# One attention place per visit, with the outputs in G1's PSUM banks, in a fused retention and MLP kernel

## The chip, the core and the metric

The kernel runs on one core of a Trainium2 chip. The metric is the device time of one execution in microseconds; lower is better. TensorE (PE in the profile) multiplies matrices into PSUM, VectorE (DVE) and ScalarE (ACT) read PSUM and write SBUF, GpSimd (POOL) works on SBUF and issues the loads, and SyncE (SP) issues the stores.

## The reference

```python
# q, k, v: 8 batches x 8 heads x 576 positions x 64
scores = scale * np.matmul(q, k.transpose(0, 1, 3, 2))
Dmat = np.where(rel >= 0, gamma[:, None, None] ** rel[None, :, :], 0.0)   # rel = i - j
ret = scores * Dmat[None, :, :, :]
attn_out = np.matmul(ret, v)
x = attn_out.transpose(0, 2, 1, 3).reshape(8 * 576, 512)     # 4608 tokens
h = x @ w_in                                                 # 512 -> 2048
g = h * np.tanh(log1p(exp(h)))                               # Mish
out = g @ w_out                                              # 2048 -> 512
```

The decay of a head is a power of the distance, so earlier positions enter a block through a running state (the sum of k times v), and only pairs within a block need scores.

## The kernel before

**Chunks and tiles.** Each batch is cut into blocks of 128 positions; the last 64 positions of two batches share a block. That gives 36 chunks of 128 tokens. The first 8 are the first blocks of the 8 batches and need no state. Then, for each pair of batches, come three blocks of each and the shared one. Four chunks make a tile of 512 tokens, so there are 9 tiles.

**Steps of a chunk n** (`att(n, steps)`):
- P (L273): VectorE scales q into one half of the tile qks; k is loaded straight into the other half.
- V (L279): GpSimd scales v into vs.
- T: transposes q and k into qkT. For chunks below NPE = 18, TensorE does it (L288, eight 128x128 matmuls) and ScalarE copies the result (L289). From 18 on it is a DMA transpose in SyncE's queue (L291).
- S (L301): 16 small matmuls with 64 rows of weights give the scores in two PSUM banks (pool ps_sc, tile sc). VectorE multiplies them by the mask into sm (L305).
- O: 16 matmuls add state times q (L353; twice as many in the first half for the shared block) and vs times sm (L358). The result is a part of xT, the MLP's input.

`state(upto)` runs at most one step of the states, and nothing where chunk `upto` already has its state: eight matmuls with 64 columns of weights (L333) add into the bank st, which VectorE then reads out to ssb (L336). The first step of a batch reads the tile k0, the others a chunk's qks and vs.

**Per tile of tokens.** `g1(t, f)` multiplies 128 of the 2048 hidden columns: four 128x512 matmuls (L371) into one of two banks (pool ps_h, tile hp), and ScalarE applies Mish (L373). `g2(t, i)` is a quarter of a 128-token output: four 128x512 matmuls (L386) into the one bank ops (pool ps_o). After the fourth quarter the result waits in `ready`, and the next `stores()` has VectorE copy it (L422) and SyncE send it off.

**PSUM.** The eight banks are: two scores tiles of two banks, one st, two hp and one ops.

**Order.** All engines run in the order in which the code issues (manual schedule). After a start-up for the first two tiles, the main loop has phases t = 2 to 9, each with 16 steps i. In a step, G1 of tile t runs ahead of a quarter of G2 of tile t-1; in phase 2, G2 (of tile 1) runs in every second step only, and phase 9 has no G1. Eight steps are a visit (w = i % 8) and serve two chunks, n and n+1, of tile t+1: n = 12, 14 in phase 2, 16, 18 in phase 3, and so on up to 34 in phase 7. Phase 8 has no attention. Before the change a visit has two attention places: the scores of n and n+1 at w = 0 and their outputs at w = 4. In both kernels a quarter that ends an output of G2 falls on w = 3 and w = 7 from phase 3 on, so `stores()` has work at w = 4 and w = 0.

**Where outputs go.** In phase 1 `step_o` (tile index 2) uses the bank ops; later ones use the first bank of the chunk's own scores tile, which the product has emptied. VectorE casts them to xT (L362).

**Buffers that matter.** qks has nine buffers, qkT five, vs five, sm three, ssb six, the stored result four.

Of the kernel before, what the change touches and what calls it, by code (L numbers as in the profile page):

```python
# [10 lines left out]
F32 = mybir.dt.float32  # L11
# [6 lines left out]
def kernel(  # L18
# [18 lines left out]
    nc = tc.nc  # L37
    B, H, S, D = q.shape
    assert (B, H, S, D) == (8, 8, 576, 64)
    P = 128  # L40
    NP = H // 2
# [5 lines left out]
    NPE = 18  # L47
# [10 lines left out]
    n_chunks = len(chunks)  # L58
# [15 lines left out]
    ps_h = ctx.enter_context(tc.tile_pool(name="ps_h", bufs=2, space=PS))  # L74
    ps_o = ctx.enter_context(tc.tile_pool(name="ps_o", bufs=1, space=PS))
# [94 lines left out]
    xts = {}  # L170
# [76 lines left out]
    def load_k0(b):  # L247
        k0[b] = first.tile([P, H, D], BF16, name="k0", bufs=B)
        nc.gpsimd.dma_start(out=k0[b], in_=k[b, :, 0:P, :].rearrange("h p d -> p h d"))
# [69 lines left out]
    def state(upto):  # L319

        if upto >= n_chunks or done[0] > state_of[upto]:
            return False
        b, c = states[done[0]]
        done[0] += 1
        if c == 0:
            ks, vs = k0[b], v0s[b]
            st_ps[b] = ps_st.tile([P, NP, 64], F32, name="st")
        else:
            ks, vs = live[index[b, c]]["qks"][:, 1], live[index[b, c]]["vs"]
        st = st_ps[b]  # L330
        for p in range(NP):
            for e in range(2):
                nc.tensor.matmul(st[ds(64 * e, 64), p, :], lhsT=ks[:, 2 * p + e, :], rhs=vs[:, 2 * p + e, :],  # L333
                                 start=(c == 0 and p == 0), stop=True, skip_group_check=True)
        ssb = tr.tile([P, 2, NP, 64], BF16, name="ssb", bufs=6)
        nc.vector.tensor_tensor(  # L336
            ssb.rearrange("p e n d -> p e (n d)"),
            st.rearrange("p n d -> p (n d)").unsqueeze(1).to_broadcast([P, 2, NP * 64]),
            diag.unsqueeze(2).to_broadcast([P, 2, NP * 64]), op=OP.mult)
        st_sb[b, c] = ssb  # L340
        return True

    def step_o(n):
        b, c = chunks[n]
        t, s = divmod(n, NCH)
        assert done[0] > state_of[n]
        qk, vs, sc, sm = (live[n][x] for x in ("qk", "vs", "sc", "sm"))
        ot = ps_o.tile([P, NP, P], F32, name="ops") if t == 2 else sc[:, 0]
        halves = [(0, P, b, c - 1)] if c < 4 else [(0, 64, b, 3), (64, 64, b + 1, 3)]
        for i0, iw, bb, cc in halves:  # L350
            for p in range(NP):
                for e in range(2):
                    nc.tensor.matmul(ot[ds(64 * e, 64), p, ds(i0, iw)], lhsT=st_sb[bb, cc][:, e, p, :],  # L353
                                     rhs=qk[:, 0, p, ds(i0, iw)],
                                     start=(i0 == 0 and p == 0), stop=False, skip_group_check=True)
        for p in range(NP):
            for e in range(2):
                nc.tensor.matmul(ot[ds(64 * e, 64), p, :], lhsT=vs[:, 2 * p + e, :], rhs=sm[:, e, p, :],  # L358
                                 start=False, stop=True, skip_group_check=True)
        if s == 0:  # L360
            xts[t] = xp.tile([P, KC, NCH * P], BF16, name="xT")
        nc.vector.tensor_copy(xts[t][:, :, ts(s, P)], ot)  # L362

    outs = {}

    def g1(t, f, cols=slice(0, NCH * P)):
        if t not in gts:
            gts[t] = gp.tile([P, nF, NCH * P], BF16, name="gT")
        hp = ps_h.tile([P, NCH * P], F32, name="hp")
        for c in range(KC):  # L370
            nc.tensor.matmul(hp[:, cols], lhsT=w_in_t[:, c, ts(f, P)], rhs=xts[t][:, c, cols],  # L371
                             start=(c == 0), stop=(c == KC - 1))
        nc.scalar.activation(gts[t][:, f, cols], hp[:, cols], AX.Mish)  # L373

    def g2(t, i):
        s, part = divmod(i, 4)
        if t == nT - 1:
            s = (s + 3) % 4
        if part == 0:
            if (t == nT - 1 and s % 2) or (t == 1 and s < 2):  # L380
                outs[t] = ps_h.tile([P, d_model], F32, name="hp")
            else:
                outs[t] = ps_o.tile([P, d_model], F32, name="ops")
        ops = outs[t]
        for f in range(4 * part, 4 * part + 4):
            nc.tensor.matmul(ops, lhsT=gts[t][:, f, ts(s, P)], rhs=w_out_t[:, f, :],  # L386
                             start=(f == 0), stop=(f == nF - 1))
        if part == 3:
            ready.append((t, s, ops))
# [3 lines left out]
    def stores():  # L393
        while ready:
            store(*ready.pop(), nc.vector.tensor_copy)
# [24 lines left out]
    def store(t, s, ops, copy):  # L420
        ot = op.tile([P, d_model], F32, name="res")
        copy(ot, ops)  # L422
        b, c = chunks[NCH * t + s]
        if c < 4:
            nc.sync.dma_start(out=out[ds(b * S + P * c, P), :], in_=ot)
        else:
            for e in range(2):
                nc.sync.dma_start(out=out[ds((b + e) * S + 512, 64), :], in_=ot[ds(64 * e, 64), :])

    def att(n, steps):  # L430
        if n >= n_chunks:
            return
        for step in steps:
            {"P": step_p, "V": step_v, "T": step_t, "S": step_s, "O": step_o}[step](n)

    dve, act, pool = nc.vector.tensor_copy, nc.scalar.copy, nc.gpsimd.tensor_copy
# [63 lines left out]
    for i in range(nF):  # L500
        for step in steps.get(i, "").split():
            n = int(step[1])
# [17 lines left out]
    def more_loads(upto):  # L520
        for _ in range(2):
            if queued[0] <= upto:
                load(queued[0])
                queued[0] += 1
# [4 lines left out]
    for u in range(24):  # L529
        j, w = divmod(u, 4)  # L530
# [32 lines left out]
    for t in range(2, nT + 1):  # L563
        for i in range(nF):
            n, w = NCH * (t + 1) + i // 8 * 2, i % 8
            if t in (3, 4) and i in (4, 12):
                load_k0(2 * t - 2 + i // 8)
            by_pe = n + 2 < NPE
            if w == 0:
                stores()  # L570
                state(n + 1)
                att(n, "S")
                att(n + 1, "S")
            if w == 4:
                state(n + 3)
                stores()
                att(n, "O")
                att(n + 1, "O")
                state(n + 3)
            if by_pe and w in (1, 3):  # L580
                att(n + 2 + w // 2, "P")
            if w in (0, 1):
                att(n + 2 + w, "V")
            if w in (4, 5):
                more_loads(n + w - 2 + PF)
            if w - (5 if by_pe else 0) in (0, 1):
                att(n + 2 + (w == 1 or w == 6), "T")
            if w == 7 and n + 4 >= NPE:
                att(n + 4, "P")
                att(n + 5, "P")  # L590
            stores()
            if t < nT:
                g1(t, i)
            if t == 2:
                if i % 2:
                    g2(1, 8 + i // 2)
            elif t < nT or i < 12:
                g2(t - 1, i)
# [32 lines left out]
```

## Time and profile before

| | us |
|---|---|
| median of three runs | 312.92 (312.32 to 312.98) |
| the profiled execution: its own time | 313.61 |
| its span in the trace | 311.9 |
| TensorE busy | 300.3 |
| VectorE, ScalarE, GpSimd busy | 137.1, 110.7, 143.6 |
| G1 matmuls (L371) busy | 141.3, x562 |
| G2 matmuls (L386) busy, into ops and hp | 110.1 and 14.7 |
| the 24 casts of L362 from sc | 15.3, 0.68 each |

How to read it: a line of a timeline begins with the start in microseconds from the span's start and a busy time, then the engine, the source line, the operation, what it writes and reads, and how many instructions are merged; in square brackets stands the idle time ahead and what ended it. Matmuls overlap and their ends are modelled, so lengths on TensorE are read from start to start. A few matmul records are missing (x3 where four were issued).

### The profile page before, as it was taken

What the parts mean: (1) busy time and instruction counts of PE and PEld (TensorE: products, weight loads), DVE (VectorE), ACT (ScalarE), POOL (GpSimd) and SP (SyncE); (2) the same over time, 40 slices, a digit from 0 to 9 for tenths busy, and PEclk for the clock granted to TensorE, in tenths of its full rate; (3) what the DMA queues carried; (4) which work ended last, traced back from release to release, by engine and by line L of the source; (5) the groups of instructions that cost most, each with busy time, mean ns of one, the idle gap of its engine ahead of it and who ended that gap; (6) DMA issues with size and microseconds to landing.
All of it is one profiled execution on the core that took longest, in us unless ns stands there. A gap on an engine that the chain in (4) does not pass through costs nothing.

```text
span 311.9 us, 5809 instructions
## 1 busy us (share of the span) xinstructions
PE 300.3 (96%) x2429; PEld 152.3 (49%) x2468; DVE 137.1 (44%) x200; ACT 110.7 (36%) x183; POOL 143.6 (46%) x178
## 2 busy tenths in 40 slices
PE   7769999999999999999999999999999999999995
PEld 3444554555465554545454444545454544444444
DVE  4723455778637635443434453535354332001111
ACT  4546345671453623233333333232323333333300
POOL 8578849989985976274726262612010000000000
PEclk9999999999999999999999999999999999999999
DMA  7999999999995999999996949371504100010031
GB/s 177 234 206 205 220 208 221 256 171 175 232 203 96 148 181 191 155 195 146 179 178 116 189 88 218 77 144 37 101 36 101 36 34 36 35 34 34 36 101 68
DMA packets 73642, 42.85 MB, mean 137 GB/s; under 512 B 58640, under 2 KB 64528, under 8 KB 73616
## 3 DMA queue, kind: packets, MB, share of 16 engines
q0 software_dynamic: 48640, 27.27, 61.1%
q1 hardware_dynamic: 24832, 15.08, 23.3%
q8 instruction: 19, 0.31, 0.5%
q10 hardware_dynamic: 144, 0.13, 0.1%
q14 instruction: 7, 0.06, 0.1%
HBM read 38.80 MB, written 9.44 MB: 155 GB/s over the span
## 4 chain that ended last, share of the span: by engine, by line
PE 92%; issue 2%; DMA 2%; POOL 2%; DVE 0%; ACT 0%; POOLq 0%; ACTq 0%
PE hp L371 39%; PE ops L386 30%; PE hp L386 4%; PE sc L301 3%; PE st L333 3%; DMA gT<-in_v_dram 2%; PE hp L403 2%; PE sc L353 2%; PE sc L358 2%; PE sc L288 1%; PE st L403 1%; PE ops L403 1%; PE hp L414 1%; POOL gT L106 1%; POOL vb L222 1%
## 5 line engine op out<-in xcount | busy, mean ns | idle before, releaser
L371 PE MATMUL hp<-xT,w_in_t 128*128 128x512 bf16 (+1 forms) x562 | 141.3, 373 | 2.2 <-DVE xT L239 0.8
L373 ACT ACTIVATE gT<-hp 128x512 bf16<-128x512 f32 (+1 forms) x148 | 86.8, 586 | 156.4 <-PE hp L371 144.2
L386 PE MATMUL ops<-w_out_t,gT 128*128 128x512 bf16 x430 | 110.1, 379 | 0.4
L371 PEld LDWEIGHTS <-w_in_t 128*128 128x128 bf16 x592 | 55.1, 98 | 61.9 <-DVE xT L239 1.3
L386 PEld LDWEIGHTS <-gT 128*128 128x128 bf16 x496 | 48.2, 98 | 58.1 <-issue 0.8
L422 DVE COPY res<-ops 128x512 f32<-128x512 f32 x28 | 19.3, 688 | 82.7 <-PE ops L386 79.7
L279 POOL TENSOR_TENSOR vs<-vraw,gv 128x512 bf16<-128x512 f32 x28 | 30.3, 1096 | 51.8 <-PE sc L358 37.6
L336 DVE TENSOR_TENSOR ssb<-st,diag 128x512 bf16<-128x512 f32 x32 | 21.9, 685 | 47.2 <-PE st L333 47.2
L305 DVE TENSOR_TENSOR sm<-sc,mask 128x1024 bf16<-128x1024 f32 x28 | 33.0, 1215 | 6.2 <-PE sc L301 6.2
L263 POOL DMA_DIRECT2D qraw<-in_q_dram x24 | 21.8, 910 | 12.8 <-DVE qks L273 9.6
L263 POOL DMA_DIRECT2D vraw<-in_v_dram x24 | 21.8, 908 | 2.9 <-DMA vpair<-in_v_dram 1.5
L263 POOL DMA_DIRECT2D qks<-in_k_dram x24 | 21.8, 906 | 1.3 <-DMA w_out_t<-in_moe_w_out_dram 0.9
L273 DVE TENSOR_TENSOR qks<-qraw,gq 128x512 bf16<-128x512 f32 x28 | 20.2, 758 | 0.0
L362 DVE CAST xT<-sc 128x512 bf16<-128x512 f32 x24 | 15.3, 680 | 0.0
L386 PE MATMUL hp<-w_out_t,gT 128*128 128x512 bf16 x61 | 14.7, 379 | 0.2
L289 ACT COPY qkT<-sc 128x1024 bf16<-128x1024 bf16 x10 | 10.1, 1010 | 8.0 <-PE sc L288 8.0
L215 DVE TENSOR_TENSOR sm<-sc,dmask 128x1024 bf16<-128x1024 f32 x8 | 9.4, 1220 | 5.0 <-PE sc L211 5.0
L353 PE MATMUL sc<-qkT,ssb 128*64 128x128 bf16 (+1 forms) x224 | 9.5, 213 | 0.0
L358 PE MATMUL sc<-sm,vs 128*64 128x128 bf16 x192 | 9.4, 219 | 0.0
L301 PE MATMUL sc<-qkT 64*128 64x128 bf16 x224 | 9.0, 218 | 0.0
L403 PEld LDWEIGHTS <-gT 128*128 128x128 bf16 x64 | 5.8, 98 | 6.5
L267 POOL DMA_DIRECT2D qraw<-in_q_dram x8 | 5.6, 706 | 7.3 <-DVE qks L273 7.3
(103 smaller groups left out, 192.0 us busy)
## 6 DMA issues: line engine op xcount, KB each, us to landing
out_dram<-res SPq DMA_DIRECT2D x31, 256.0 KB, 3.0
qraw<-in_q_dram POOLq DMA_DIRECT2D x24, 256.0 KB, 6.0
vraw<-in_v_dram POOLq DMA_DIRECT2D x24, 256.0 KB, 6.8
qks<-in_k_dram POOLq DMA_DIRECT2D x24, 128.0 KB, 6.4
w_in_t<-in_moe_w_in_dram POOLq DMA_DIRECT2D x4, 512.0 KB, 11.1
w_out_t<-in_moe_w_out_dram POOLq DMA_DIRECT2D x4, 512.0 KB, 9.8
gT<-in_q_dram SPq DMA_DIRECT2D x4, 256.0 KB, 4.9
gT<-in_k_dram POOLq DMA_DIRECT2D x8, 128.0 KB, 6.3
```

The costliest lines, as they stand in the source:

```text
L263: nc.gpsimd.dma_start(out=t, in_=src[b, :, ds(P * c, P), :].rearrange("h p d -> p h d"))
L273: nc.vector.tensor_tensor(live[n]["qks"][:, 0], live[n]["q"], gq[:, c, :].unsqueeze(2).to_broadcast([P, H, D]), op=OP.mult)
L279: nc.gpsimd.tensor_tensor(vs, live[n]["v"], gv[:, c, :].unsqueeze(2).to_broadcast([P, H, D]), op=OP.mult)
L301: nc.tensor.matmul(sc[:, e, p, :], lhsT=qk[r, 1, p, :], rhs=qk[r, 0, p, :], start=True, stop=True)
L305: nc.vector.tensor_tensor(sm.rearrange("p e n i -> p (e n) i"), sc.rearrange("p e n i -> p (e n) i"), m.unsqueeze(1).to_broadcast([P, 2 * ...
L336: nc.vector.tensor_tensor(ssb.rearrange("p e n d -> p e (n d)"), st.rearrange("p n d -> p (n d)").unsqueeze(1).to_broadcast([P, 2, NP * 64 ...
L353: nc.tensor.matmul(ot[ds(64 * e, 64), p, ds(i0, iw)], lhsT=st_sb[bb, cc][:, e, p, :], rhs=qk[:, 0, p, ds(i0, iw)], start=(i0 == 0 and p == ...
L371: nc.tensor.matmul(hp[:, cols], lhsT=w_in_t[:, c, ts(f, P)], rhs=xts[t][:, c, cols], start=(c == 0), stop=(c == KC - 1))
L373: nc.scalar.activation(gts[t][:, f, cols], hp[:, cols], AX.Mish)
L386: nc.tensor.matmul(ops, lhsT=gts[t][:, f, ts(s, P)], rhs=w_out_t[:, f, :], start=(f == 0), stop=(f == nF - 1))
L403: nc.tensor.matmul(outs[0, s], lhsT=gts[0][:, f, ts(s, P)], rhs=w_out_t[:, f, :], start=(f == 0), stop=(f == nF - 1))
L422: copy(ot, ops)
```

## The change

A visit keeps one attention place, at w = 6: a state, the outputs of n and n+1, another state, then the scores of n+2 and n+3, and a third state where one is due. The first scores (chunks 12 and 13) stay at the start of phase 2. From chunk 12 on, outputs go into two hp banks, and ScalarE casts them. Transposes on TensorE move from w = 5 and 6 to w = 2 and 4. The DMA transposes of n+4 and n+5 go to w = 7 and to w = 0 of the next visit, where those of n+2 and n+3 were at w = 0 and 1; the scaling P of n+4 and n+5 moves from w = 7 to w = 4 and 5. What is computed stays the same, and so does the number of instructions on TensorE.

```diff
@@ step_o
-        ot = ps_o.tile([P, NP, P], F32, name="ops") if t == 2 else sc[:, 0]
+        pool, name = (ps_o, "ops") if t == 2 else (ps_h, "hp")
+        ot = pool.tile([P, NP, P], F32, name=name)
...
-        nc.vector.tensor_copy(xts[t][:, :, ts(s, P)], ot)
+        (nc.vector.tensor_copy if t == 2 else nc.scalar.copy)(xts[t][:, :, ts(s, P)], ot)
@@ main loop
-            by_pe = n + 2 < NPE
-            if w == 0:
+            if t == 2 and i == 0:
                 stores()
                 state(n + 1)
                 att(n, "S")
                 att(n + 1, "S")
-            if w == 4:
-                state(n + 3)
-                stores()
+                state(n + 1)
+            if w == 6:
+                state(min(n + 4, n_chunks - 1))
                 att(n, "O")
                 att(n + 1, "O")
+                state(min(n + 4, n_chunks - 1))
+                att(n + 2, "S")
+                att(n + 3, "S")
                 state(n + 3)
-            if by_pe and w in (1, 3):
+            if w in (1, 3) and n + 2 < NPE:
                 att(n + 2 + w // 2, "P")
+            if w in (4, 5) and n + 4 >= NPE:
+                att(n + w, "P")
             if w in (0, 1):
                 att(n + 2 + w, "V")
             if w in (4, 5):
                 more_loads(n + w - 2 + PF)
-            if w - (5 if by_pe else 0) in (0, 1):
-                att(n + 2 + (w == 1 or w == 6), "T")
+            if w in (2, 4) and n + 2 < NPE:
+                att(n + 1 + w // 2, "T")
             if w == 7 and n + 4 >= NPE:
-                att(n + 4, "P")
-                att(n + 5, "P")
+                att(n + 4, "T")
+            if w == 0 and n + 2 >= NPE:
+                att(n + 3, "T")
             stores()
```

## Prediction

> **What bounds the kernel now.** I read the page first: the engines, then the chain that ended last.
>
> ```profile
> PE 300.3 (96%) x2429; PEld 152.3 (49%) x2468; DVE 137.1 (44%) x200; ACT 110.7 (36%) x183; POOL 143.6 (46%) x178
> ...
> PE 92%; issue 2%; DMA 2%; POOL 2%; DVE 0%; ACT 0%; POOLq 0%; ACTq 0%
> ```
>
> TensorE is busy 96% of the span and is 92% of the chain; no other engine reaches half. So the change is worth only what it does to TensorE's gaps, and gaps of hundredths of a microsecond, repeated per visit, are the whole matter. The granted clock is 1.00 in every stretch from 80 us on, so one price per matmul holds. I therefore read TensorE's timeline by the starts of its groups. In the steady phases groups of four 512-column matmuls (G1 on L371, G2 on L386) start 0.863 us apart. Everything above that at an attention place is the place's price. One visit of before, with the outputs first and the scores 8 us later:
>
> ```profile
> 129.39 1.03 PE L386 MATMUL ops<-w_out_t,gT 128*128 128x512 bf16 x4
> 130.35 0.32 PE L333 MATMUL st<-vs,qks 128*64 128x64 bf16 x8
> ...
> 131.17 0.39 PE L358 MATMUL sc<-sm,vs 128*64 128x128 bf16 x8
> 131.54 0.32 PE L333 MATMUL st<-vs,qks 128*64 128x64 bf16 x8
> 131.79 1.04 PE L371 MATMUL hp<-xT,w_in_t 128*128 128x512 bf16 x3
> ...
> 137.84 1.03 PE L386 MATMUL ops<-w_out_t,gT 128*128 128x512 bf16 x4
> 138.80 0.62 PE L301 MATMUL sc<-qkT 64*128 64x128 bf16 x16
> 139.36 0.82 PE L371 MATMUL hp<-xT,w_in_t 128*128 128x512 bf16 x3
> ```
>
> The reader is to see three things. The G2 group ahead of a place takes 0.96 us (129.39 to 130.35, 137.84 to 138.80) instead of 0.86: 0.10 for going from 128x128 weights to halves of the array. The scores take 0.55 (138.80 to 139.36). The second state starts 1.19 after the first.
>
> **The merge.** A scores place alone costs 137.84 to 139.36, 1.52, less the group's 0.86: 0.66. What scores cost when they follow a state is shown where a state stands ahead of them in before:
>
> ```profile
> 121.58 1.03 PE L386 MATMUL ops<-w_out_t,gT 128*128 128x512 bf16 x4
> 122.54 0.32 PE L333 MATMUL st<-vs,qks 128*64 128x64 bf16 x8
> 122.78 0.62 PE L301 MATMUL sc<-qkT 64*128 64x128 bf16 x16
> 123.34 1.04 PE L371 MATMUL hp<-xT,w_in_t 128*128 128x512 bf16 x3
> ```
>
> The state lasts 0.25 there, as it does when G1 follows it (131.54 to 131.79), and the scores 0.55 again. So behind the second state of an output place the scores add 0.55, and each merge saves 0.66 - 0.55 = 0.11 (an entry of 0.10 and 0.01 in the first G1 group behind it). Of the 12 visits (chunks 12 to 34), 11 have scores to bring along; in the order of the changed kernel 8 of them hold two states: 8 x 0.107 = 0.86 us saved. (0.107 by starts in nanoseconds.)
>
> The Trainium skill, page "TensorEngine Tiling (Array Packing)", section "Key Properties", says that a change of tiling mode drains the array, and "TensorE: Matmul & The Clock Gate", section "Single matmul latency", puts the fixed part of a warm matmul at about 166 ns. By that estimate the 8 merges would save 1.4 and the final sum would be some 0.5 lower. I take the 0.10 of the rows, which are of just these shapes.
>
> **Three visits with a third state.** Before, three scores places have a state ahead of them, as above, at 121.58 to 123.34 less 0.86 = 0.90. In the changed order that state comes last, behind the scores (chunks 16, 22 and 30). It writes the one st bank, so it must wait until VectorE has read the second state out. VectorE does that in 0.69:
>
> ```profile
> 130.70 0.69 DVE L336 TENSOR_TENSOR ssb<-st,diag 128x512 bf16<-128x512 f32 x1 [4.51 <-PE st L333]
> ```
>
> From one state's start to the next one's this wait makes 1.19 where the second reads qks (130.35 to 131.54), and 1.10 where it reads k0 (114.18 to 115.28). Behind the second state lie only 0.25 + 0.55 = 0.80 of state and scores, so TensorE stands for 0.30 to 0.39. The place grows by 1.10 or 1.19 and loses the 0.90 elsewhere: +0.29, +0.20 (chunk 22, a k0) and +0.29, together +0.78. Queued behind the waiting state are G1 and all else of TensorE. The scores' products wait on VectorE behind the second ssb, but need some 3.4 us in all and have 4.3 until the next copy of ops, so they delay nothing.
>
> **The ops bank loses its cover.** This is the largest term. G2 has one PSUM bank (ops); every fourth step VectorE must copy it before G2 may start again. In phases 3 to 7 that falls on steps with w = 0 and w = 4, and there before puts exactly its two attention places between the old group and the new one. The change empties both and moves all to w = 6. Then only one G1 group, 0.86, lies between. Phase 8 of before, which has no attention left, shows that case:
>
> ```profile
> 266.77 1.03 PE L371 MATMUL hp<-xT,w_in_t 128*128 128x512 bf16 x4
> 267.72 1.02 PE L386 MATMUL ops<-w_out_t,gT 128*128 128x512 bf16 x4
> ```
>
> ```profile
> 266.98 0.69 DVE L422 COPY res<-ops 128x512 f32<-128x512 f32 x1 [6.17 <-PE ops L386]
> ```
>
> 266.77 to 267.72 is 0.95, not 0.86: the copy starts 0.04 behind the last matmul's end, takes 0.69, and G2 starts 0.05 after it. The four turnovers there cost 0.083, 0.082, 0.081 and 0.082. Five phases with four turnovers each are newly bare: 20 x 0.082 = 1.64 us added. (Phase 2 runs two G1 groups between and keeps its cover.) Bounds: nothing, if the copy were ready sooner; 0.13, if its start lagged by 0.09 as one copy of before did (matmul end 106.68, start 106.77).
>
> **Outputs in G1's banks, copied by ScalarE.** The cast takes 0.585 on ScalarE (row of the groups by line, below) against 0.68 on VectorE.
>
> ```profile
> L239 ACT CAST xT<-hp 128x512 bf16<-128x512 f32 x1 | 0.6, 585 | 1.3 <-PE hp L236 1.3
> ```
>
> Counted from the place's start, the first output's matmuls end at 0.86; with 0.04, 0.585 and 0.05 its bank is free at 1.54. G1 wants it at 2.0 or later, behind the other output, the second state and the scores: hidden, with 0.45 to spare. The second copy ends at 2.1, and its bank is wanted 0.86 (phase 2) or 1.73 later. The Mish behind the copies then starts on time. On the other side, the second output needs the bank of the G1 group before last; its Mish ends about when the place begins, 0.7 ahead of need. Only the last place (chunks 34 and 35) has neither states nor scores as cover: in before it runs from 258.72 to 259.86, its first output ends at 259.45, and 259.45 + 0.68 = 260.12, so +0.27. If the cover were gone everywhere, 11 x 0.27 more.
>
> On VectorE 24 casts of 0.68 disappear. The page "TensorEngine Tiling (Array Packing)", section "PSUM Bottleneck", advises ScalarE and VectorE together for emptying PSUM. Here VectorE stood idle for 3.8 us or more before the copies of w = 0 and for 6.2 before the bare ones of phase 8, so its casts held nobody: booked at nothing.
>
> **Transposes, products and loads.** PE transposes (0.45 each, eight 0.056 matmuls) move from w = 5, 6 to 2, 4 in phase 2 without any mode change. DMA transposes move past one output store in SyncE's queue; the first of a pair leaves when its qks is scaled, the second once the first output of the place has read its buffer.
>
> ```profile
> DMA to landing us min/median/max: 3.1/6.0/11.8
> ```
>
> From that output to the scores of the next place are over 14 us, against 11.8 at worst: nothing. VectorE's scaling moves to w = 4, 5, ahead of a store; in its queue it follows the store of w = 0 and runs then, on loads that landed long before (chunk 18's at 88 us, for a product at about 96). GpSimd's vs waits two steps longer for the outputs but no longer for the scaling; its next loads leave about as before, and are wanted some 25 us later. Both at nothing; each microsecond that one lacks would be TensorE's.
>
> **Sum.** -0.86 + 0.78 + 1.64 + 0.27 = +1.83 us. The profiled execution takes 313.61 (span 311.9 and 1.7 around it) and would become 315.4; it lies 0.7 above the median of the three runs. On the median 312.92 the forecast is 314.8. About 0.2%, 0.6 us, can be told from no change here.
>
> **Rivals.**
> 1. Faster: VectorE's round trip shortens as its casts leave, and the bare copies and third states cost less. Each turnover shortens by x up to 0.08, each third state by x up to 0.4. It decides at x = 0.08: -0.86 + 0 + 0.54 + 0.27 = -0.05; at x = 0.4 the time is 312.92 - 0.86 - 0.3 + 0.27 = 312.0. For it: 24 casts fewer. Against: the copies already found VectorE idle. Faster 0.05, between the two 0.06.
> 2. Slower still: a transpose pair lands after its scores are due. It decides at about 14 us of landing; the first pairs took 9.5 to 11.8 while the DMA engines were 90% busy, and now start closer to the loads. One or two late pairs at 1 to 2 us: 316 to 318. Chance 0.06.
> 3. Slower still: ScalarE's copies come late in every visit. It decides beyond 0.45 us of delay; 11 visits at 0.1 to 0.3 give 1 to 3 us: 316 to 318. Against: ScalarE is idle 1.13 before every Mish. Chance 0.06.
> The forecast has 0.77. Its own bounds: turnovers at 0.05 and third states at 0.5 in all give 313.9; turnovers at 0.13 give 315.8. The range 313.7 to 315.9 leaves out the two slow rivals and most of the first. Chances: faster 0.05, same 0.06, slower 0.89.
>
> **What would show it.** G2's first matmul at w = 0 and w = 4 of phases 3 to 7 starts 0.95 after the G1 group's first, not 0.86: the main step. In 8 places the scores follow the second state at 0.25 and last 0.55. In three places the last state starts 0.3 to 0.4 behind the scores' end. G1 behind the last place is 0.27 later. A G1 group that waits on ScalarE in an ordinary place, scores that wait on a transpose, or turnovers at 0.86 would make the prediction wrong.

## The result, and the profile after

The changed kernel takes 315.64 us (median of six runs, 315.03 to 316.39), the kernel before 312.74 on the same chip (six runs, 312.23 to 313.39): ratio 1.0095, 95% interval 1.0075 to 1.0115. The forecast was 314.8, in a range of 313.7 to 315.9. The profiled execution took 315.03, with a span of 313.3 and a granted clock of 1.00. The engines and the chain, from the page after:

```profile
PE 303.4 (97%) x2468; PEld 153.2 (49%) x2468; DVE 125.8 (40%) x176; ACT 123.8 (40%) x207; POOL 143.0 (46%) x178
...
PE 90%; issue 2%; DMA 2%; DVE 2%; POOL 2%; ACT 1%; POOLq 0%; DVEq 0%; ACTq 0%
```

The 24 casts have gone from VectorE (x200 before) to ScalarE (x183 before), and TensorE is still the bound. That TensorE's busy time rose from 300.3 says little, as 2468 of its matmul records are in this trace and 2429 were in the one before. What did change is the chain: VectorE now holds 2% of it and ScalarE 1%, where both rounded to 0%.

The time ahead of phase 2 varies by up to 3 us between executions (in the ten that were profiled, its first G1 group started between 79.0 and 82.0 us), so single executions are compared by a stretch that leaves it out: from that first G1 group to the start of the last G2 group of phase 8. It takes 213.51 us before and 216.20 after, **+2.69** (the medians differ by 2.90). Gap by gap over the starts of TensorE's groups, it splits as follows.

| | forecast | found |
|---|---|---|
| eight merges | -0.86 | -0.86 |
| three third states | +0.78 | +0.77 |
| bare turnovers of ops, phases 3 to 7 | +1.64 | +1.64 |
| last place | +0.27 | +0.26 |
| transposes, products, loads | 0 | +0.97 |
| second state of chunk 14's place | - | -0.09 |
| sum | +1.83 | +2.69 |

TensorE's timeline after, with the turnover of w = 0 and then a whole place of w = 6:

```profile
113.64 1.03 PE L372 MATMUL hp<-xT,w_in_t 128*128 128x512 bf16 x4
114.59 1.02 PE L387 MATMUL ops<-w_out_t,gT 128*128 128x512 bf16 x4
...
133.88 0.32 PE L333 MATMUL st<-vs,qks 128*64 128x64 bf16 x8
...
135.08 0.32 PE L333 MATMUL st<-vs,qks 128*64 128x64 bf16 x8
135.32 0.62 PE L301 MATMUL sc<-qkT 64*128 64x128 bf16 x16
135.88 1.04 PE L372 MATMUL hp<-xT,w_in_t 128*128 128x512 bf16 x4
```

VectorE's, at that turnover:

```profile
113.84 0.69 DVE L423 COPY res<-ops 128x512 f32<-128x512 f32 x1 [5.54 <-PE ops L387]
```

The reader is to see the copy stand bare between two groups: G1 to G2 takes 0.95 (113.64 to 114.59) instead of 0.86, exactly as phase 8 did before, and VectorE had stood idle for 5.54 before the copy. In the place, the scores follow the second state at 0.25 and last 0.55 (135.077, 135.325 and 135.877 before rounding), so the merge gives what it promised. A place with a third state:

```profile
118.62 0.62 PE L301 MATMUL sc<-qkT 64*128 64x128 bf16 x16
119.56 0.32 PE L333 MATMUL st<-vs,qks 128*64 128x64 bf16 x8 [0.32 <-DVE ssb L336]
119.81 1.04 PE L372 MATMUL hp<-xT,w_in_t 128*128 128x512 bf16 x4
```

Scores to state takes 0.94 here instead of 0.55. TensorE stands for VectorE's reading of st, 0.32 of it marked in brackets. The last place, TensorE and then ScalarE:

```profile
264.17 0.39 PE L359 MATMUL hp<-sm,vs 128*64 128x128 bf16 x8
264.76 1.02 PE L372 MATMUL hp<-xT,w_in_t 128*128 128x512 bf16 x4 [0.20 <-ACT xT L363]
```

```profile
264.12 1.07 ACT L363 CAST xT<-hp 128x512 bf16<-128x512 f32 x2 [0.84 <-PE hp L359]
```

Of the places after phase 2's start, this is the only one where a G1 group waits for ScalarE's cast: 0.59 from the last output to G1, where 0.33 was enough before (the G1 group itself then takes 0.01 less).

The gap that was not foreseen is at the second step of phase 2, ahead of the first transpose on TensorE (chunk 14). TensorE first, then VectorE:

```profile
80.83 1.03 PE L387 MATMUL ops<-w_out_t,gT 128*128 128x512 bf16 x4
82.66 0.62 PE L288 MATMUL sc<-ident,qks 128*128 128x128 bf16 x8 [0.81 <-DVE qks L273]
```

```profile
78.45 0.69 DVE L423 COPY res<-hp 128x512 f32<-128x512 f32 x1 [1.85 <-ACT qkT L289]
79.06 0.68 DVE L336 TENSOR_TENSOR ssb<-st,diag 128x512 bf16<-128x512 f32 x1
79.66 2.34 DVE L305 TENSOR_TENSOR sm<-sc,mask 128x1024 bf16<-128x1024 f32 x2
81.92 1.28 DVE L273 TENSOR_TENSOR qks<-qraw,gq 128x512 bf16<-128x512 f32 x2
```

The transpose reads qks, which the scaling P (L273) writes. P's loads had landed by 71.2, but it stands in VectorE's queue behind a copy, an ssb and two products, and its first instruction starts only at 81.92 (x2: chunks 14 and 15). TensorE's G2 group would have been followed at 81.69 (80.83 and 0.86); the transpose starts at 82.66, 0.97 later.

One gap became shorter without having been forecast, in the place of chunk 14: from its first state to its second, before and then after.

```profile
98.99 0.32 PE L333 MATMUL st<-vs,qks 128*64 128x64 bf16 x8
100.19 0.32 PE L333 MATMUL st<-vs,qks 128*64 128x64 bf16 x8
```

```profile
102.10 0.32 PE L333 MATMUL st<-vs,qks 128*64 128x64 bf16 x8
103.20 0.32 PE L333 MATMUL st<-vs,qks 128*64 128x64 bf16 x8
```

It takes 1.10 instead of 1.20, though its second state reads qks, for which the prediction had 1.19. VectorE's reading of st starts as far behind the first state in both (at 99.35 and 102.45, 0.36 and 0.35 behind it) and takes 0.69 in both. e4 and e7, which lighten VectorE in the order of before, keep the 1.20, so the missing casts are not the cause; what it is stays open.

The DMA transposes came sooner too, from a median of 6.0 us and 11.8 at worst to this (the issues of L291 after):

```profile
DMA to landing us min/median/max: 3.0/3.1/5.6
```

### The profile page after: what moved, and what is told of

Read it like the earlier page. It is cut to its first block, busy times and chain, and to the rows that moved or that the text cites. A ratio compares the mean times of both kernels' runs of the same rounds, so it can differ in the third digit from the quotient of the medians.

```text
span 313.3 us, 5859 instructions
## 1 busy us (share of the span) xinstructions
PE 303.4 (97%) x2468; PEld 153.2 (49%) x2468; DVE 125.8 (40%) x176; ACT 123.8 (40%) x207; POOL 143.0 (46%) x178
## 4 chain that ended last, share of the span: by engine, by line
PE 90%; issue 2%; DMA 2%; DVE 2%; POOL 2%; ACT 1%; POOLq 0%; DVEq 0%; ACTq 0%
PE hp L372 39%; PE ops L387 30%; PE hp L387 4%; PE st L333 3%; PE hp L404 2%; DMA gT<-in_v_dram 2%; PE sc L301 2%; PE hp L354 2%; PE hp L359 2%; PE sc L288 1%; PE st L404 1%; PE ops L404 1%; PE hp L415 1%; DVE sm L305 1%; DVE ssb L336 1%
## 5 line engine op out<-in xcount | busy, mean ns | idle before, releaser
L372 PE MATMUL hp<-xT,w_in_t 128*128 128x512 bf16 (+1 forms) x592 | 143.6, 373 | 1.1 <-DVE xT L239 0.8
L372 PEld LDWEIGHTS <-w_in_t 128*128 128x128 bf16 x592 | 56.1, 98 | 64.0 <-DVE xT L239 1.3
L263 POOL DMA_DIRECT2D vraw<-in_v_dram x24 | 21.8, 909 | 2.5 <-DMA vpair<-in_v_dram 1.5
L263 POOL DMA_DIRECT2D qraw<-in_q_dram x24 | 21.8, 907 | 2.4 <-DMA vpair<-in_v_dram 1.5
L273 DVE TENSOR_TENSOR qks<-qraw,gq 128x512 bf16<-128x512 f32 x28 | 21.0, 762 | 0.1
L363 ACT CAST xT<-hp 128x512 bf16<-128x512 f32 x24 | 12.9, 588 | 11.5 <-PE hp L359 11.5
L354 PE MATMUL hp<-qkT,ssb 128*64 128x128 bf16 (+1 forms) x224 | 9.5, 213 | 0.0
L359 PE MATMUL hp<-sm,vs 128*64 128x128 bf16 x192 | 9.4, 219 | 0.0
L333 PEld LDWEIGHTS <-qks 128*64 128x64 bf16 x192 | 5.1, 110 | 7.3 <-issue 6.0
```

The lines of the kernel that those rows point to most:

```text
L263: nc.gpsimd.dma_start(out=t, in_=src[b, :, ds(P * c, P), :].rearrange("h p d -> p h d"))
L273: nc.vector.tensor_tensor(live[n]["qks"][:, 0], live[n]["q"], gq[:, c, :].unsqueeze(2).to_broadcast([P, H, D]), op=OP.mult)
```

## The experiments

The theory was that the difference is a sum of four small waits on TensorE (20 bare turnovers, three third states, the late P, the last place) less the merges, each to be taken away alone. The rivals were that the waits share one cause (a busier VectorE or ScalarE), so that removing one moves it elsewhere, and that the sooner transposes or the banks of the outputs pay by themselves. The kernel before took 313.11 (25 runs) beside the first four experiments and 312.93 (35 runs) beside the last four. "Stretch" is the one above.

### e1_p14: the first scaling ahead of the products

```diff
                 state(n + 1)
+                att(n + 2, "P")
                 att(n, "S")
...
-            if w in (1, 3) and n + 2 < NPE:
+            if w in (1, 3) and n + 2 < NPE and (t, i) != (2, 1):
```

> The changed kernel, with the scaling P of chunk 14 issued ahead of the first scores of phase 2, so that VectorE does it before the two products and not behind them. Theory: in the changed kernel the first PE transpose of phase 2 stood for 0.97 us because it waited for this scaling, which ended 0.06 before it started. Then the stand goes and the stretch from phase 2 to the end shrinks from +2.69 to +1.72 us against before (about 314.5). Rival: the transpose waited for its scores bank, which the product of chunk 12 empties. That product now ends 0.68 later, so the stand stays or shifts and the time does not fall.

Measured: 314.74 us (313.89 to 317.42), ratio 1.0036 (1.0004 to 1.0068); stretch 215.21, 0.99 less than the changed kernel's. TensorE, then VectorE, at the same step:

```profile
80.99 1.03 PE L387 MATMUL ops<-w_out_t,gT 128*128 128x512 bf16 x4
81.85 0.61 PE L288 MATMUL sc<-ident,qks 128*128 128x128 bf16 x8
```

```profile
79.82 0.68 DVE L273 TENSOR_TENSOR qks<-qraw,gq 128x512 bf16<-128x512 f32 x1
80.42 2.35 DVE L305 TENSOR_TENSOR sm<-sc,mask 128x1024 bf16<-128x1024 f32 x2
```

P now runs ahead of the products, the transpose follows G2 at 0.86, and the products, 0.76 later, delay nobody. VectorE does the same work as in the changed kernel, so the whole 0.97 was its order.

### e2_act_stores: ScalarE copies the results of G2

```diff
     ready = []
+    ready_by = [0]
...
-            store(*ready.pop(), nc.vector.tensor_copy)
+            store(*ready.pop(), nc.scalar.copy if ready_by[0] else nc.vector.tensor_copy)
...
+    ready_by[0] = 1
     for t in range(2, nT + 1):
```

> The changed kernel, with ScalarE instead of VectorE copying ops from phase 2 on. Theory: a bare turnover costs 0.082 us because the copy of 0.69 and its 0.04 + 0.05 of signals last longer than one G1 group of 0.863. At 0.585 on ScalarE they last less, so all 24 bare turnovers (20 new ones and the 4 of phase 8) vanish: -1.97 us. VectorE also loses one copy ahead of the first products, which shortens the stand of the first transpose by about 0.4. In all about -2.4 against the changed kernel: +0.3 against before, 313.0. Rival: a turnover costs what it costs for other reasons (the change of bank itself, the weights): then 0.08 stay and the time falls by 0.4 at most.

Measured: 313.73 us (313.14 to 316.26), ratio 1.0026 (0.9993 to 1.0058); stretch 214.16, 2.04 less than the changed kernel's. TensorE and ScalarE at a turnover:

```profile
125.05 1.03 PE L372 MATMUL hp<-xT,w_in_t 128*128 128x512 bf16 x4
125.93 1.02 PE L387 MATMUL ops<-w_out_t,gT 128*128 128x512 bf16 x4
```

```profile
125.29 0.59 ACT L424 COPY res<-ops 128x512 f32<-128x512 f32 x1 [0.31 <-PE ops L387]
126.11 0.60 ACT L374 ACTIVATE gT<-hp 128x512 bf16<-128x512 f32 x1 [0.23 <-PE hp L372]
```

G1 to G2 is 0.88 here. ScalarE's copy starts 0.04 later than VectorE's did (0.24 behind the G1 group's start instead of 0.20) but takes 0.585 instead of 0.69, so 0.018 remains of each 0.082 (the first two of phase 3 vanish whole), and the Mish behind it (126.11) still finds ScalarE idle. All 24 bare turnovers together (20 new, four of phase 8) went from 2.04 to 0.40; the other 0.40 is the late P, which moved up by one copy in VectorE's queue and stood 0.57 instead of 0.97. The miss is the 0.018 that is left. The expectation set 0.69 + 0.04 + 0.05 against the 0.863, but that is only 0.78; it leaves out that the copy starts 0.20 (VectorE) or 0.24 (ScalarE) behind the G1 group's start. With that the sums are 0.20 + 0.69 + 0.05 = 0.94 for VectorE and 0.24 + 0.585 + 0.05 = 0.88 for ScalarE. Otherwise the turnovers are bank waits on VectorE's copy, as the prediction priced them.

### e3_third_later: the third state two groups behind the scores

```diff
                 att(n + 3, "S")
+            if w == 7:
                 state(n + 3)
```

> The changed kernel, with the third state of three visits moved one step on, to a place of its own at w = 7. Theory: behind the scores it stood 0.30 to 0.39 us for VectorE's reading of the st bank; a step later the bank is free, and the state costs an entry of 0.09, 0.25 and 0.01, that is 0.35 in place of 0.55 to 0.64 above the scores. Three visits: -0.29, -0.19, -0.29, together -0.77 us (about 314.9). Rival: the stand is the price of going back from scores to states; then it stays with the entry and nothing is gained.

Measured: 315.66 us (314.63 to 317.97), ratio 1.0077 (1.0043 to 1.0111); stretch 215.60, 0.60 less than the changed kernel's. TensorE, the same place:

```profile
119.01 0.62 PE L301 MATMUL sc<-qkT 64*128 64x128 bf16 x16
119.56 1.04 PE L372 MATMUL hp<-xT,w_in_t 128*128 128x512 bf16 x3
120.43 1.03 PE L387 MATMUL ops<-w_out_t,gT 128*128 128x512 bf16 x4
121.39 0.32 PE L333 MATMUL st<-vs,qks 128*64 128x64 bf16 x8
121.64 1.04 PE L372 MATMUL hp<-xT,w_in_t 128*128 128x512 bf16 x4
```

The wait on st is gone. The state now pays its own entry (G2 takes 0.96 ahead of it) and its 0.25. The three places gave back the 0.77 expected; in this execution 0.17 of it was lost at the late P, which stood 1.14 instead of 0.97. The times alone could not have told this: the interval overlaps that of the changed kernel.

### e4_outputs_alone: before, with outputs in G1's banks

```diff
-        ot = ps_o.tile([P, NP, P], F32, name="ops") if t == 2 else sc[:, 0]
+        pool, name = (ps_o, "ops") if t == 2 else (ps_h, "hp")
+        ot = pool.tile([P, NP, P], F32, name=name)
...
-        nc.vector.tensor_copy(xts[t][:, :, ts(s, P)], ot)
+        (nc.vector.tensor_copy if t == 2 else nc.scalar.copy)(xts[t][:, :, ts(s, P)], ot)
```

> The kernel before, with only the outputs put into the hp banks and cast by ScalarE; places and orders as before. Theory: without scores behind the outputs the first G1 group comes 1.44 us (second state reads k0, 4 places) or 1.54 us (7 places) after the place's start, and the first output's bank is free at 1.54. So the casts cost about 0.1 in four places, nothing to 0.03 in seven, and 0.27 in the last: +0.7 us, 313.5. Rival: VectorE was the limit, and its 24 casts of 0.68 fewer make the kernel faster than before.

Measured: 324.04, 322.94, 314.59 and 323.31 us. The profiled execution is the one of 324.04: TensorE stood long for two DMA transposes, and behind that wait its granted clock was 0.50 for some 4 us. The other three have no trace, so there is no ratio, and only 314.59 is near the kernel before. On TensorE, the price of the outputs, and then what stopped this execution:

```profile
114.37 0.32 PE L333 MATMUL st<-v0s,k 128*64 128x64 bf16 x8
114.71 1.02 PE L372 MATMUL hp<-xT,w_in_t 128*128 128x512 bf16 x3
...
123.08 0.40 PE L301 MATMUL sc<-qkT 64*128 64x128 bf16 x8 [1.06 <-DMA qkT<-qks]
130.83 0.61 PE L301 MATMUL sc<-qkT 64*128 64x128 bf16 x8 [7.35 <-DMA qkT<-qks]
```

State to G1 is 0.34 instead of 0.25 in four places with a k0 state and 0.28 in two more, since no scores lie there to hide ScalarE's casts; the last place has its +0.27. That comes to about +0.7, as expected. So in the changed kernel it is the scores behind the outputs that hide the casts. The 8.4 us for chunks 18 and 19 (1.06 and 7.35 in the brackets) are another matter: two DMA transposes landed 15.9 and 21.8 us after issue. Why just here is not settled, and the time of the experiment stays inconclusive.

### e5_transposes_alone: before, with the transposes sooner

```diff
-            if w - (5 if by_pe else 0) in (0, 1):
-                att(n + 2 + (w == 1 or w == 6), "T")
+            if by_pe and w in (5, 6):
+                att(n + w - 3, "T")
+            if w in (4, 5) and n + 4 >= NPE:
+                att(n + w, "P")
             if w == 7 and n + 4 >= NPE:
-                att(n + 4, "P")
-                att(n + 5, "P")
+                att(n + 4, "T")
+            if w == 0 and not by_pe:
+                att(n + 3, "T")
```

> The kernel before, with only the DMA transposes and their scaling moved as in the change (scaling at w = 4 and 5, transposes at w = 7 and 0). Theory: TensorE's order is untouched, so the undisturbed time stays that of before within 0.3 us (312.5 to 313.2); the transposes leave ahead of the loads and land 3 to 6 us after issue, not 9.5 to 11.8, so that scores never wait for them and the executions of before at 314 to 315.5 become rarer. Rival: transposes were never late; then landing times change and neither time nor scatter does. A second rival: sooner transposes hold up the loads, and vs or the scaling comes late; then it is slower by 1 us or more.

Measured: 313.53 us (312.71 to 315.89), ratio 1.0009 (0.9973 to 1.0045); stretch 214.16, 0.65 more than before. The issues of L291, and TensorE at a scores place:

```profile
DMA to landing us min/median/max: 3.0/6.6/15.8
```

```profile
140.43 0.40 PE L301 MATMUL sc<-qkT 64*128 64x128 bf16 x8
141.31 0.40 PE L301 MATMUL sc<-qkT 64*128 64x128 bf16 x8 [0.48 <-DMA qkT<-qks]
```

The expectation failed: sooner by itself does not make the transposes land faster (median 6.6, before 6.0), the one that took 15.8 us made a scores place 0.65 longer, and long executions did not become rarer (three of ten above 315, before four of 35). In this kernel the first pairs still leave while loads move (119 to 124 and 136 to 143 us). In the changed kernel the second and third pair leave at 115.06, 117.89, 131.68 and 134.46, just ahead of the loads, and land in 3.1. The first pair (96.18 and 102.75) leaves while loads move, and still lands in 5.6 and 4.8. So the short landings go with the order against the loads, but the loads alone do not make the long ones. It was seen, not isolated.

### e6_scores_apart: changed, with the scores back in a place of their own

```diff
-            if t == 2 and i == 0:
+            if w == 0:
                 stores()
-                state(n + 1)
+                if t == 2 and i == 0:
+                    state(n + 1)
                 att(n, "S")
                 att(n + 1, "S")
...
                 state(min(n + 4, n_chunks - 1))
-                att(n + 2, "S")
-                att(n + 3, "S")
-                state(n + 3)
```

> The changed kernel, with the scores (and the third states behind them) back in a place of their own at w = 0, outputs and states left at w = 6. Theory: against the changed kernel, 8 entries of 0.107 come back (+0.86); the 10 turnovers at w = 0 get their cover again (-0.83); the three third states wait for nothing (-0.78); and without scores behind the outputs G1 waits for ScalarE's first cast, 0.09 in four places and 0.03 in a few (+0.4 to 0.5). Sum about -0.3 us. Rival: one place is worth more than the entries (the array's change of halves costs more than the rows show); then the separate scores make the kernel slower by over 1 us.

Measured: 315.58 us (315.20 to 318.18), ratio 1.0078 (1.0045 to 1.0111); stretch 216.49, 0.29 more than the changed kernel's, where 0.3 less was expected. The terms that were named held: entries +0.86, ten turnovers covered again -0.83, third states -0.77, G1 waiting for ScalarE's casts +0.44 (0.52 in six places, less 0.08 that the G1 groups behind them save). What was missed is a second late P, on TensorE ahead of the transpose of chunk 16:

```profile
95.23 1.03 PE L387 MATMUL ops<-w_out_t,gT 128*128 128x512 bf16 x4
96.65 0.62 PE L288 MATMUL sc<-ident,qks 128*128 128x128 bf16 x8 [0.40 <-DVE qks L273]
```

Together with the first, which stood 1.01, this costs some 0.6 more than in the changed kernel. The scores at w = 0 put their products ahead of that P, the same order as at the first one. By these terms, two places would be some 0.3 faster than one without that second late P, as expected; the products that stand ahead of P in VectorE's queue turned this round.

### e7_before_act_stores: before, with ScalarE copying the results of G2

The edit is that of e2, made to the kernel before.

> The kernel before, with ScalarE copying ops from phase 2 on. Theory: only the four turnovers of phase 8 are bare there; each falls from 0.083 to 0.018, -0.26 us in all (312.5 to 312.9). A loss would come from the outputs' place at w = 4, if ScalarE's copy held up a Mish. Rival: freeing VectorE by 28 copies of 0.69 shortens the way from state to state (1.10 to 1.19) and saves up to 11 x 0.1 more.

Measured: 314.91 us (312.42 to 317.12), ratio 1.0032 (0.9995 to 1.0068), not told from no change: seven of the ten runs lie at 314.2 or above, for which there is no trace. In the profiled execution, 312.42 and the shortest of the ten, the stretch is 213.25, 0.26 less than before, as expected: only phase 8's four turnovers are bare there and each went from 0.083 to 0.018. One of them:

```profile
265.84 1.03 PE L371 MATMUL hp<-xT,w_in_t 128*128 128x512 bf16 x4
266.73 1.02 PE L386 MATMUL ops<-w_out_t,gT 128*128 128x512 bf16 x4
```

State to state did not change, so a lighter VectorE makes no round trip shorter. ScalarE's copies gain 1.64 in the changed kernel and 0.26 in this one: the bare turnovers are the change's own cost.

### e8_all_mended: the four waits taken away together

The edits of e1, e2 and e3 on the changed kernel, and the last two outputs back in their scores tiles with VectorE's cast:

```diff
+        late = n >= n_chunks - 2
+        if late:
+            ot = sc[:, 0]
+        else:
+            pool, name = (ps_o, "ops") if t == 2 else (ps_h, "hp")
+            ot = pool.tile([P, NP, P], F32, name=name)
```

> The changed kernel with four mends: scaling of chunk 14 ahead of the first products, ScalarE copying ops, the third states at w = 7, and the last two outputs in their scores tile with VectorE's cast. Theory: the terms add up. From phase 2 to the end: +2.69 - 0.97 - 1.61 - 0.77 - 0.27 = -0.93 us against before, that is what the 8 merges (0.86), two saved entries more or less and the turnovers of phase 8 bring: about 311.9. Rival: the terms hide one another, and one of them comes back behind the next (the first transpose, a copy of ScalarE ahead of a Mish): then it stays above before.

Measured: **311.56 us** (311.32 to 314.89, twelve runs), ratio to before 0.9965 (0.9932 to 0.9998): 0.35% below the kernel before, with the end of the interval just under 1, and clearly below the changed kernel. Stretch 212.56, 0.95 less than before. TensorE, at a turnover, at a whole place, and at the last one:

```profile
128.90 1.03 PE L376 MATMUL hp<-xT,w_in_t 128*128 128x512 bf16 x4
129.78 1.02 PE L391 MATMUL ops<-w_out_t,gT 128*128 128x512 bf16 x4
...
133.65 0.32 PE L333 MATMUL st<-vs,qks 128*64 128x64 bf16 x8
133.90 0.62 PE L301 MATMUL sc<-qkT 64*128 64x128 bf16 x16
134.45 1.04 PE L376 MATMUL hp<-xT,w_in_t 128*128 128x512 bf16 x3
...
261.22 0.39 PE L363 MATMUL sc<-sm,vs 128*64 128x128 bf16 x8
261.55 1.04 PE L376 MATMUL hp<-xT,w_in_t 128*128 128x512 bf16 x3
```

Turnover 0.88, scores behind a state 0.25 and 0.55, last place 0.33. Summed from the single runs: 0.97 for P, 1.64 for the copies, 0.77 for the third states and 0.27 for the last place make 3.65 off the changed kernel's +2.69, or -0.96. So the four prices add, and the rival that the waits have one cause falls. Only the late P also moves with what stands ahead of it in VectorE's queue (e2, e3, e6).

## Why the prediction was right, and where a step failed

- **The merge** held at its price: an entry of 0.10 and 0.01 behind it, eight times. The 0.10 of the rows was the right one to take. The estimate that the prediction weighed, which takes the fixed part of a warm matmul (about 166 ns by the Trainium skill, "TensorE: Matmul & The Clock Gate", section "Single matmul latency") as the price of a change of mode, would have made the merges 1.4.
- **The third states** held in place and size: 0.39, 0.30 and 0.39 over the 0.55, and e3 takes just these away. VectorE's reading of st is what ended the wait.
- **The ops bank's cover** was the largest term, as forecast. Its size was the 1.64 of the forecast: 19 of the new turnovers are 0.080 to 0.084 each. One is 0.138, the first of phase 3, whose copy lags as it did before; the G2 group behind each is some 0.003 shorter, which gives 0.06 back, and the two cancel. e2 and e7 show the mechanism from both sides.
- **Outputs in G1's banks** cost nothing in the ordinary places and 0.27 in the last. That this rests on the scores as cover is shown by e4 and e6.
- **The step that failed** is "Transposes, products and loads", with "both at nothing". It followed the DMA transposes, the loads and the scaling from w = 4 on. It booked the transposes on TensorE in phase 2 as moved "without any mode change" and did not follow the P that the first of them reads. That transpose moved three steps sooner, to w = 2, while its P stays at w = 1, behind the products in VectorE's queue. The move used up the slack: 0.97 us, shown by e1. The rule that was kept for SyncE's queue (every queue that a moved step depends on) was not applied to VectorE's.
- **The rivals.** A shorter round trip on VectorE did not come: turnovers stayed at 0.082 and e7 left the states' spacing as it was (the 0.09 of chunk 14's place has another cause). Late DMA transposes did not come either; in the changed kernel they landed sooner. ScalarE's casts were late in no ordinary place.

Some readings of the prediction were off without consequence. Its bounds come out as 313.8 and 315.7, not 313.9 and 315.8. Before the first copy of w = 0 (106.77) VectorE had stood idle for 2.45, not 3.8 or more. ScalarE stood idle for 0.16 before one Mish of phase 2 (105.85), not 1.13. G1 came 1.90 behind the start of the places of chunks 12, 14 and 26, not 2.0 or later, which still left 0.36 to spare.

The forecast was 0.84 below the median of the changed kernel. On the stretch, the missed 0.97, less the 0.09 of chunk 14's place and 0.02 in other terms, makes the +2.69 found of the +1.83 forecast. That the time still fell into the range is in part luck: the room above the forecast was meant for turnovers of 0.13, of which only one came, and the late P, priced at nothing, used it up.

## What to carry to other kernels

When an engine is full, the work that stands between two uses of a PSUM bank is worth something even if it could be merged elsewhere: here moving it saved 0.86 us of entries and cost 1.64 in bare turnovers. When a step is moved earlier, follow what it reads back to its producer's place in that engine's queue; in an in-order queue, being ready is not being next. Waits that stand apart in the trace can be mended one by one; here their prices added up (3.65 forecast from the single runs, 3.64 found), and a change that lost as a whole came out slightly ahead once each was mended.

## What the runs showed of the hardware that was not expected

- DMA transposes that left amid the loads up to about 146 us took 9 to 22 us to land in before, e4 and e5, and those that left amid later loads 4 to 8. In the changed kernel and in e8, whose pairs from the second on leave just ahead of the loads, none took more than 5.6 and 6.6, and the longest was the very first, which left amid loads too. No run isolated what makes the difference.
- In e4, after TensorE had stood for some 8 us, its 512-column matmuls ran at 0.42 to 0.43 us apiece for some 4 us, at a granted clock of 0.50, against 0.216 in the steady phases. The three groups behind the wait lost 2.0 us by that, so the price of the wait was more than its length.
- ScalarE starts a copy of a PSUM bank 0.04 later than VectorE behind the same matmul but copies 128x512 fp32 in 0.585 instead of 0.69, which is enough to cover all but 0.018 of a turnover.
